# An attention and spectral-filter kernel: values turned and a bound summed on VectorE, low parts subtracted on GpSimd, and one filter piece's products ahead of the branch

## The chip, the cores and the metric

The kernel runs on one core of a Trainium2 chip. The metric is the time of one execution on the device, in microseconds (us); before the change it is 625.97 us, the median of 3 runs (625.66 to 625.98). The engines are TensorE (PE in the profile; its weight loads are listed as PEld), VectorE (DVE), ScalarE (ACT), GpSimd (POOL) and SyncE (SP, which only issues transfers). A name with a q behind it (PEldq, DVEq) is the engine's sequencer, which takes instructions in order, waits for their semaphores, loads registers and branches. TensorE writes to PSUM, which has eight banks of 128 x 512 float32.

## The reference

Two independent halves, put side by side. The first is attention with 16 heads of 28 columns that share one set of keys and values; the second multiplies a two-dimensional spectrum by a filter.

```python
# A: S = 2048, D = 448, H = 16, Dh = 28; wq and wk are eight times as large as the other weights
q = (x @ wq).reshape(B, S, H, Dh).transpose(0, 2, 1, 3)
k, v = x @ wk, x @ wv
p = softmax(einsum("bhqd,bkd->bhqk", q, k) * Dh ** -0.5)
a = einsum("bhqk,bkd->bhqd", p, v).transpose(0, 2, 1, 3).reshape(B, S, H * Dh) @ wo
# B: w_r, w_i of S x (D/2 + 1)
b = irfft2(rfft2(x) * (w_r + 1j * w_i), s=(S, D))
out = concatenate([a, b], axis=-1)
```

## The kernel before, in words

**Numbers in two parts.** TensorE multiplies in a fast mode that keeps fewer bits of a float32. Inputs, weights, keys and queries are therefore split into a high part (a cast) and a low part (the value less its high part, the helper `low`, L281), and a product is summed from three: high by high, high by low, low by high.

**Before the branch (about 5 to 69 us).** The input x comes in four chunks of 512 rows (c = 0 to 3) and four slices of columns (j = 0 to 3). For each chunk the high parts `xh` are cast (VectorE for c = 0, else ScalarE) and the low parts `xl` are subtracted on VectorE (L281). TensorE then makes the projections (L330): four groups of four heads, whose spare rows carry the columns of keys and values. ScalarE evicts each to `qraw` (L334) and VectorE takes the largest magnitude of each row (L335). Transfers from the SP and POOL queues gather keys and values into `kf` (L477), rows 0 to 31 the keys, 32 to 63 the values. Keys are split per half of 1024 columns: ScalarE casts (`keys_cast`, L276), VectorE subtracts (`keys_low`, L281), and SP copies the result to the three other strips of 32 partitions (`keys_strip`, L491). The first half is done ahead of the branch, the second behind it.

In between, the forward transform of the filter half runs in eight pieces q: VectorE folds the input (`fold_part`, L143 to L151), TensorE makes features from the folds (`features`, L161, one call for p = 0 and one for p = 1, each of e = 0 and 1), ScalarE copies them (L430), TensorE multiplies them by twiddles (`fft1_mm`, L171, into two banks), the result is copied out (`fft1_evict`, L186 on ScalarE or L188 on VectorE) and stored by SP (`fft1_store`, L192). Pieces 0 to 5 are done whole before the branch. Piece 6 (`L` in the code) and piece 7 have their features before it, and their L171 behind it, in `first_fill`.

**A bound per row.** Instead of the largest score of each row, the kernel subtracts a bound: the sum over a head's columns of |q| times |k| by their maxima. VectorE multiplies the maxima (`terms`, L496), TensorE sums over the 28 rows of a head with a matrix of ones and zeros `blk` (`shift`, L502), VectorE copies the sum to `cvec` (`bound`, L505), once for the first chunk and once for the other three. The largest of all sums is found by a reduce (L603), four small products that bring it to one partition (`tops`, L620), and a reduce to the single number `bits` (L621). Every engine loads `bits` into a register (`values_load`, L607) and branches (L635): where the bound is too large, a slow exact loop runs. With these inputs it does not.

**Values.** The value product wants the values with rows as keys: 16 blocks of 32 x 128 are transposed by TensorE against a unit matrix (L592: four, eight and four), collected in one bank, and copied to `vs` by VectorE behind the branch (L665).

**The order.** Before the branch each unit of work is a task with an engine, an assumed duration, the tasks it waits for and, where given, a due time. TensorE's tasks stay in the order of the code; for the other engines a small planner picks, among the tasks that could start first, the one due first. Behind the branch the order is written out by hand and by a running account of planned times (`clk`, and `free` for seven of the banks): the first strips of scores, the pieces' L171, value products, filter work.

**Behind the branch.** The scores of 512 queries and 128 keys make a step: four strips of 32 rows side by side (L1169, three products each, four banks), exponentials on ScalarE (L1185 for one bank, L1183 for two neighbours), and the value products of the step before last (L1218) into bank 7. `first_fill` puts the L171 of pieces 6 and 7 behind the first and the second step, in a free bank and bank 7, and its copies (L188) on VectorE. About 80 such steps are followed by groups in another form (L1146), mixed with the rest of the filter and the output projection (L1071). The spectrum's transform and its inverse are long chains on VectorE in the background.

## Time and profile before

| what | us |
|---|---|
| median of the runs | 625.97 |
| span of the profiled execution, first to last instruction | 624.6 |
| what the median has beyond that span | 1.37 |
| TensorE busy | 619.0 (99%) |
| ScalarE busy | 541.0 (87%) |
| VectorE busy | 344.1 (55%) |
| GpSimd busy | 90.7 (15%) |

The profiled execution's time is its span and what lies around it, for which the profile has no row of its own. A row of the timeline or of the chain gives start, length, engine, line and operation, what is written and read, and in brackets the idle time of the engine before it and what ended that. A matmul row's length is modelled and overlaps the next one. A row of the groups gives a count, the busy time, and the mean of one in ns. TensorE's granted clock is 1.00 all along.

### The profile page before, as it was taken

How to read it: one execution, taken by the hardware profiler on the slowest of the kernel's cores; microseconds unless marked ns; L12 is line 12 of the kernel's file. 1: busy time of each engine (PE TensorE's matmuls, PEld its weight loads, DVE VectorE, ACT ScalarE, POOL GpSimd, SP SyncE). 2: the span in 40 equal slices, each digit the busy share in tenths (PEclk: the TensorE clock that was granted, in tenths of full speed). 3: DMA queues.
4: the chain of work that ended last, by engine and by line, in shares of the span. 5: the costliest groups of instructions: out<-in, count | busy, mean ns of one | idle time of the engine just before them, and what ended most of it. 6: DMA issues, size and time to landing. Idle time of an engine off the chain costs nothing.

```text
span 624.6 us, 13634 instructions
## 1 busy us (share of the span) xinstructions
PE 619.0 (99%) x5367; PEld 319.4 (51%) x5367; DVE 344.1 (55%) x685; ACT 541.0 (87%) x977; POOL 90.7 (15%) x168
## 2 busy tenths in 40 slices
PE   9999999999999999999999999999999999999997
PEld 7877633333333346654345565656653346564335
DVE  6999604979698987897732513227451231321014
ACT  4645799999999998889999888878889998888993
POOL 1021130102121101020321210030210101020200
PEclk9999999999999999999999999999999999999999
DMA  8856794001123331171664242294213131016001
GB/s 304 276 134 171 193 247 185 16 20 46 34 90 88 87 76 47 40 161 28 211 213 104 77 119 78 61 215 147 82 60 94 34 98 34 16 66 149 18 1 59
DMA packets 28748, 65.31 MB, mean 105 GB/s; under 512 B 6514, under 2 KB 15826, under 8 KB 27270
## 3 DMA queue, kind: packets, MB, share of 16 engines
q1 hardware_dynamic: 21066, 43.25, 24.9%
q0 software_dynamic: 7472, 20.96, 11.3%
q8 instruction: 42, 0.69, 0.5%
q10 hardware_dynamic: 144, 0.23, 0.1%
q14 instruction: 24, 0.19, 0.1%
HBM read 30.35 MB, written 16.30 MB: 75 GB/s over the span
## 4 chain that ended last, share of the span: by engine, by line
PE 98%; ACT 1%; DMA 1%; DVE 0%; issue 0%; DVEq 0%; ACTq 0%
PE banks L1218 39%; PE banks L1146 21%; PE banks L1169 18%; PE banks L330 7%; PE banks L1071 6%; PE banks L973 2%; PE banks L161 2%; PE banks L999 2%; PE banks L171 1%; DMA raw<-xw 1%; ACT p L1185 0%; PE banks L592 0%; DVE bs L188 0%; PE banks L502 0%; ACT al L615 0%
## 5 line engine op out<-in xcount | busy, mean ns | idle before, releaser
L1203 ACT ACTIVATE p<-banks 128x512 f32<-128x512 f32 x512 | 256.5, 702 | 39.4 <-PE banks L1218 18.3
L1218 PE MATMUL banks<-p,vs 128*32 128x512 f32 x2048 | 254.5, 600 | 0.2 <-DVE bs L188 0.2
L1185 ACT ACTIVATE p<-banks 128x512 f32<-128x512 f32 x262 | 145.5, 614 | 1.5 <-PE banks L1169 1.2
L1146 PE MATMUL banks<-qa,ka 128*128 128x512 f32 x512 | 145.7, 407 | 0.0
L1183 ACT ACTIVATE p<-banks 128x1024 f32<-128x1024 f32 x125 | 129.3, 1034 | 0.0
L1146 PEld LDWEIGHTS banks<-qa,ka 128*128 128x128 f32 x512 | 90.6, 188 | 53.3 <-ACT p L1203 34.5
L1218 PEld LDWEIGHTS banks<-p,vs 128*32 128x32 f32 x2048 | 49.3, 108 | 112.4 <-issue 108.7
L1028 DVE COPY qraw<-banks 128x512 f32<-128x512 f32 x15 | 10.4, 691 | 68.6 <-PE banks L1218 68.6
L1033 POOL DMA_DIRECT2D sd<-qraw x15 | 8.9, 596 | 244.1 <-DVE qraw L1028 244.1
L1075 DVE COPY ya<-banks 128x448 f32<-128x448 f32 x12 | 7.5, 624 | 52.2 <-PE banks L1071 36.4
L1041 POOL DMA_DIRECT2D R<-rd x60 | 30.4, 513 | 39.4 <-DMA rd<-rs 36.5
L1169 PE MATMUL banks<-qa,oh 32*128 32x512 f32 x384 | 35.6, 443 | 0.0
L1169 PE MATMUL banks<-qa,kh 32*128 32x512 f32 x384 | 35.5, 443 | 0.0
L856 DVE SCALAR_TENSOR_TENSOR X<-w,X 128x226 f32<-128x226 f32 (+2 forms) x72 | 34.1, 473 | 2.4
L1169 PEld LDWEIGHTS banks<-qa,kh 32*128 32x128 f32 x384 | 14.5, 183 | 40.3 <-ACT p L1185 40.3
L1169 PEld LDWEIGHTS banks<-qa,oh 32*128 32x128 f32 x384 | 14.6, 183 | 38.5 <-ACT p L1185 37.7
L981 DVE CAST zh<-banks 113x512 fp32r<-113x512 f32 (+1 forms) x16 | 11.0, 685 | 27.9 <-ACT p L1203 27.0
L1005 DVE COPY w<-banks 128x256 f32<-128x256 f32 x16 | 6.8, 423 | 35.0 <-PE banks L999 31.9
L334 ACT ACTIVATE qraw<-banks 128x512 f32<-128x512 f32 x16 | 9.4, 599 | 17.8 <-PE banks L330 17.7
L330 PE MATMUL banks<-xh,wqh 128*128 128x512 f32 x64 | 24.3, 412 | 0.2 <-DVE xh L278 0.2
L1071 PE MATMUL banks<-woh,oh 128*128 128x448 f32 x64 | 23.6, 369 | 0.0
L1071 PE MATMUL banks<-wol,oh 128*128 128x448 f32 x64 | 23.1, 362 | 0.0
(139 smaller groups left out, 754.6 us busy)
## 6 DMA issues: line engine op xcount, KB each, us to landing
xb<-xb SPq DMA_DIRECT2D x8, 512.0 KB
qa<-qa SPq DMA_DIRECT2D x8, 512.0 KB
ob<-yo SPq DMA_DIRECT2D x16, 256.0 KB
X<-t POOLq DMA_DIRECT2D x8, 452.0 KB, 15.5
wf<-w POOLq DMA_DIRECT2D x8, 452.0 KB, 3.9
c<-t POOLq DMA_DIRECT2D x8, 452.0 KB, 4.4
R<-rd POOLq DMA_DIRECT2D x60, 56.0 KB, 2.4
t<-bs SPq DMA_DIRECT2D x14, 226.0 KB
```

Of the source, the lines that this page charges most:

```text
L161: mm(pa[r0:r0 + 32, e, 113 * k:113 * k + 113], f[:, 2 * r + k, 2 * p + e, h], cs1[:, 2 * r + k], start=True, stop=True)
L330: mm(pq[c, g], w[:, j, gs], x[:, j], start=(j == 0 and n == 0), stop=(j == 3 and n == 1))
L856: todo(226 * n, lambda d=d, q=q: STT(both(d), t[0].rearrange("p r n f -> p r (n f)"), q, both(a), op0=ALU.mult, op1=ALU.add))
L973: mm(pz[:w, j], fb["c2", q % 2][:, e, j, :w], fb["fi", q % 2][:, j], start=True, stop=True)
L1041: nc.gpsimd.dma_start(R[32 * i:32 * i + DH], rd[i:i + 1].to_broadcast([DH, CW]))
L1071: mm(p, x[c][:, g, s], w[:, m], start=(g == 0 and n == 0), stop=(g == NG - 1 and n == 2))
L1146: mm(bank[b], ka[:, kc * 128:(kc + 1) * 128], qa[c, g][:, h], start=True, stop=True)
L1169: mm(bank[bs[i]], k[r, kc * 128:(kc + 1) * 128], q[r], start=(n == 0), stop=(n == 2))
L1183: nc.scalar.activation(ends[1], banks[:, bs[1]:bs[1] + 2], AF.Exp, scale=SCALE)
L1185: nc.scalar.activation(pt[4 * st + i], bank[bs[i]], AF.Exp, scale=SCALE)
L1203: nc.scalar.activation(p, bank[b], AF.Exp, scale=SCALE)
L1218: mm(bank[7][32 * i:32 * i + 32], vs[:, kc], pt.pop(4 * st + i), start=(kc == 0), stop=(kc == 15))
```

## The change

Turning the values and summing the bound leave TensorE. VectorE transposes in blocks of 32 x 32: four instructions turn blocks 0 to 11 ahead of the branch, four small ones the last four behind it, straight into `vs`. The bound is a transpose, a sum, and a transpose back; the largest of the last result needs one product in `tops` instead of four. GpSimd subtracts the low parts of the third and fourth chunk (slices 0 to 2) and of both halves of the keys. The L171 of piece 6 moves from `first_fill` to the end of the work ahead of the branch; its copy and its two stores come first behind the branch. The products of piece 5 now stand before the features of piece 7, and these features' last part is split around `tops`: e = 0 ahead of it, the register load and e = 1 behind it. The constant `blk` and its load are gone, the starting values of `clk` and `free` are changed.

```diff
-            l = add(DVE, 0.61, lambda: low(out, lambda: xr[c, j][r], lambda: xs[c][0][r, j]), h)
+            pool = c > 1 and j < 3
+            l = add(POOL if pool else DVE, 1.6 if pool else 0.61,
+                    lambda: low(out, ..., nc.gpsimd if pool else nc.vector), h)
 ...
         def keys_low(h):
-            low(lambda: kl[:32, hs], lambda: kf[:32, hs], lambda: kh[:32, hs])
+            low(lambda: kl[:32, hs], lambda: kf[:32, hs], lambda: kh[:32, hs], nc.gpsimd)
 ...
-        def shift(c0, c1):
-            pb = small[c0] = spin(NG, c1 - c0)
-            mm(pb.rearrange("p g c -> p (g c)"), cons["blk"], prod[:, :, c0:c1], start=True, stop=True)
-        def bound(c0, c1):
-            nc.vector.tensor_copy(cvec[:, :, c0:c1], small[c0])
+        def shift(c0, c1, due, *deps):
+            def go():
+                terms(c0, c1)
+                nc.vector.transpose(across, prods)
+                nc.vector.tensor_reduce(sums[:, DH:DH + 1], across[:, :DH], axis=AX.X, op=ALU.add)
+                nc.vector.transpose(shifts, sums)
+                if c0:
+                    nc.vector.tensor_reduce(cmax, shifts, axis=AX.X, op=ALU.max)
+            return add(DVE, 0.85 if c0 else 0.65, go, kmb_, *smz, *deps, *(reds[a, b] for a in range(c0, c1) for b in range(NG)), due=due)
 ...
-                    kd = add(DVE, 1.1, lambda: keys_low(0), kc)
+                    kd = add(POOL, 3.0, lambda: keys_low(0), kc)
 ...
-        ts = add(DVE, 0.2, lambda: terms(1, NC), ...)
-        def turn_values(bs):
-            for b in bs:
-                nc.tensor.transpose(turned[0][:, b], kf[32:64, b * 128:(b + 1) * 128], cons["ident"][32:64, 32:64])
-        tv = add(PE, 0.3, first_values, ...)
-        cv = small_bank(0.2, lambda: shift(1, NC), 0.16, lambda: bound(1, NC), ts, blk_, tv)
+        fm_task(L - 1)
+        def turn_values(a, c0, c1):
+            x = kf[32:64, 128 * c0:128 * c1].rearrange("p (c a k) -> p a c k", a=4, k=32)
+            nc.vector.transpose(vs[32 * a:32 * a + 32, c0:c1], x[:, a])
+        cm = shift(1, NC, 60.0, cv0)
+        for a in range(4):
+            add(DVE, 0.5, lambda a=a: turn_values(a, 0, 12), *krow_, *fetched["v"][:7], cm if a == 3 else None)
         fa_task(L + 1, 0)
-        def last_values():
-            small["rv"] = nc.values_load(bits.bitcast(I32)[0:1, 0:1])
-            ...
-            features(pas[L + 1, 1], ff[L + 1], fc["cs1"][:113], 1)
-            turn_values(range(12, 16))
+        def last_features(e):
+            if e:
+                small["rv"] = nc.values_load(bits.bitcast(I32)[0:1, 0:1])
+            else:
+                ...
+            features(pas[L + 1, 1], ff[L + 1], fc["cs1"][:113], 1, (e,))
 ...
         def tops():
-            for g in range(NG):
-                mm(pb[0:1, 4 * g:4 * g + 4], cmax[:, g:g + 1], cons["sel4"], start=True, stop=True)
-        fm_task(L - 1)
-        tv = add(PE, 0.61, lambda: turn_values(range(4, 12)), fm[L - 1])
+            mm(pb[0:1, 0:4], cmax, cons["sel4"], start=True, stop=True)
+        lv = add(PE, 0.43, lambda: last_features(0), fa[L + 1][0], users[-6])
+        bt_ = small_bank(0.15, tops, 0.15, lambda: nc.vector.tensor_reduce(bits, small["t"][0:1, 0:4], axis=AX.X, op=ALU.max), cm, sel4_)
+        low_q["deps"].append(bt_)
-        lv = add(PE, 0.9, last_values, tv, kc, bt_, ...)
+        lv = add(PE, 0.43, lambda: last_features(1), bt_, lv)
         add(ACT, 0.5, last_evict, lv, kc)
+        add(PE, 0.85, lambda: pbs.update({L: fft1_mm(L)}), lv, *outs[L - 1])
 ...
-        nc.vector.tensor_copy(vs, turned[0])
+        fft1_out(L, pbs[L])
         keys_low(1)
+        for a in range(4):
+            turn_values(a, 12, 16)
         for p in (1, 2, 3):
             keys_strip(1, p)
 ...
-    clk = {"pe": 0.0, "dve": 1.9, ...}
-    free[turned[1]], free[turned[2]] = 0.8, 0.4
+    clk = {"pe": 0.0, "dve": 2.3, ...}
+    free[last_bank[0]], free[6] = 0.4, 0.9
 ...
-            if k < 2:
-                first_fill(L + k)
+            if not k:
+                first_fill(L + 1)
```

## The prediction

> **What bounds the kernel now.** I read the page's chain by engine first, then the chain in order of time around the branch.

> ```profile
> PE 98%; ACT 1%; DMA 1%; DVE 0%; issue 0%; DVEq 0%; ACTq 0%
> ```

> TensorE (PE) holds 98% of the chain. So a TensorE instruction taken away counts in full, unless TensorE then waits for something it did not wait for before. The rows of the chain from the last projection to the first strip of scores (start, us, what):

> ```profile
> 59.70 0.32 PE banks L502 x2
> ...
> 62.62 1.69 PE banks L161 x64
> 64.31 0.36 PE banks L592 x4
> 64.67 0.32 PE banks L502 x2
> 64.99 0.90 PE banks L161 x31
> 65.90 0.17 PE banks L620 x7
> 66.07 0.92 PE banks L171 x16
> 67.00 0.61 PE banks L592 x8
> 67.60 0.96 PE banks L161 x32
> ...
> 68.58 0.56 ACT al L615
> ...
> 69.17 0.98 PE banks L1169 x10
> ```

> The reader is to see that each piece begins where the last ends: no idle TensorE here. L592 turns the values, L502 sums the bound, L620 finds its top, L171 makes a filter piece's products, L161 their features, L1169 the first strip. The last four turnings (L592) are missing: from 68.56 to 69.17 the chain goes through ScalarE's copy of the last features (L615), and they lie beside that.

> What stands between the top of the bound and the branch is a register load, by line and in order of time:

> ```profile
> L607 PEldq TENSOR_LOAD <-bits x1: 986/986/986, 66.3 to 66.3; - x1
> L635 DVEq EVENT_SEMAPHORE  x1: 21/21/21, 68.0 to 68.0; - x1
> ...
> 65.73 0.35 PE L620 MATMUL banks<-sel,cmax 128*1 128x4 f32 x8
> 66.11 0.16 DVE L621 TENSOR_REDUCE bits<-banks 1x1 f32<-1x16 f32 x1
> ```

> The bits are written at 66.27, TensorE's sequencer loads them at once, and that takes 0.99 us, until 67.29. Nothing of it shows as idle time, because 24 matmuls (L171 and eight of L592, 1.53 us) had been handed to the array already. The whole way from the first L620 matmul to the end of the load is 1.56 us, and this cover is what the change rearranges.

> Behind the branch, ScalarE and TensorE:

> ```profile
> 69.52 1.20 DVE L281 TENSOR_TENSOR kl<-kf,kh 32x1024 fp32r<-32x1024 f32 x1
> 70.14 4.76 ACT L1185 ACTIVATE p<-banks 128x512 f32<-128x512 f32 x9 [1.00 <-PE banks L1169]
> 72.17 1.21 PE L171 MATMUL banks<-al,fwl 64*64 64x226 f32 x16
> 73.25 1.16 DVE L188 COPY bs<-banks 128x452 f32<-128x452 f32 x2 [0.91 <-ACT p L1185]
> 73.31 0.51 PE L1169 MATMUL banks<-qh,kh 32*128 32x512 f32 x4
> 74.47 1.06 PE L1218 MATMUL banks<-p,vs 128*32 128x512 f32 x8 [0.19 <-DVE bs L188]
> 74.79 1.02 ACT L1183 ACTIVATE p<-banks 128x1024 f32<-128x1024 f32 x1
> 76.95 1.02 ACT L1183 ACTIVATE p<-banks 128x1024 f32<-128x1024 f32 x1
> ...
> 78.85 1.02 ACT L1183 ACTIVATE p<-banks 128x1024 f32<-128x1024 f32 x1
> 80.82 1.02 ACT L1183 ACTIVATE p<-banks 128x1024 f32<-128x1024 f32 x1
> 81.72 1.10 ACT L1185 ACTIVATE p<-banks 128x512 f32<-128x512 f32 x2
> 82.72 1.02 ACT L1183 ACTIVATE p<-banks 128x1024 f32<-128x1024 f32 x1
> ```

> From 70.14 on ScalarE evicts without a break. Its step of four banks costs 0.90 for the double (80.82 to 81.72) and 1.00 for two singles (to 82.72), 1.90 together, the cadence of the steps (80.82 to 82.72). So TensorE and ScalarE run level here. The start is rougher: from 70.14 to 74.79 nine singles took 4.65 where 9 x 0.50 = 4.50 would do, the next steps took 2.16, 1.90 and 1.97. That is 0.15 + 0.26 + 0.07 = 0.48 us lost behind the branch, where two filter pieces are squeezed between the strips and the first value products (L1218) wait for the second one's copy (L188).

> **The change part by part.** *Taken off TensorE, ahead of the first strip:* L502 twice, 0.32 + 0.32; the turnings, 0.36 + 0.61 + 0.36 (the last four as the first four); L620 from four products to one, three quarters of 0.17, 0.12. Sum 2.09 us.

> *Moved:* the seventh piece's L171, 0.92, from behind the first strip to ahead of it. Its bank wait is for ScalarE's copies of the piece before, now made about 2 us earlier. Its two stores go ahead of the key strips on SP's queue.

> *The load's cover.* In the new order TensorE has: fifth piece's L171, features, half of the last features, the top, load, other half, the moved L171, branch. All that covered the load now stands before the top or behind the load. The load, two matmuls' latency and the bits' reduce are in the open: 1.56 less the 0.12 that two passes instead of eight save and the 0.05 that those two take, so 1.39 us idle. Bounds: nothing, if the matmuls behind the load did not wait for it, and 1.6. I take 1.39, since TensorE's queue is one queue in order and 0.99 is its own row. What queues behind the load: 32 matmuls and the branch; what waits for them: ScalarE's last feature copy, VectorE's piece copy, the first strip.

> *First strip:* 69.17 - 2.09 + 1.39 + 0.92 = 69.39, 0.22 later than before.

> *Behind it:* one filter piece fewer stands between the first strip and the value products. On TensorE that gives back 1.14 (72.17 to 73.31): L1218 at 74.47 + 0.22 - 1.14 = 73.55, 0.92 earlier. On ScalarE it can give back only the 0.48 of rough steps: 0.48 - 0.22 = 0.26 earlier. Both have the same cadence in the steps that follow, so the gain lies from 0.26 to 0.92, nearer to ScalarE's end, since ScalarE is the one without idle time here. I take 0.40. If the piece's copy were late again, L1218 would be the next to wait, as it is now.

> *Low parts on GpSimd.* Rows of the groups, then two windows (start:end, length, busy us of PE, PEld, DVE, ACT, POOL):

> ```profile
> L281 DVE TENSOR_TENSOR xl<-raw,xh 128x512 fp32r<-128x512 f32 x12 | 8.1, 686 | 0.3 <-ACT xh L276 0.2
> L281 DVE TENSOR_TENSOR kl<-kf,kh 32x1024 fp32r<-32x1024 f32 x2 | 2.4, 1202 | 0.0
> L1359 POOL TENSOR_TENSOR ol<-qraw,oh 128x128 fp32r<-128x128 f32 x3 | 1.4, 459 | 25.4 <-ACT oh L1356 25.4
> L236 POOL MEMSET kf<- 64x2048 f32 x1 | 1.8, 1802 | 0.1
> L258 POOL MEMSET wql<- 64x512 f32 x1 | 0.5, 519 | 0.3 <-POOLq L1474 0.3
> L1352 DVE STREAM_SHUFFLE r<-qraw 128x128 f32<-128x128 f32 x4 | 1.2, 301 | 0.0
> ```
> ```profile
> 16.00:57.00 41.00, 41.00 (x510) 32.24 (x508) 38.72 (x74) 21.89 (x41) 4.17 (x8) 1.00 0.65 192
> 80.00:90.00 10.00, 10.00 (x111) 3.43 (x108) 1.02 (x2) 10.00 (x17) 3.31 (x7) 1.00 1.03 249
> ```

> The two memsets give a fixed 0.09 us. With it, 459 ns is 2.87 ns a column, so 512 columns are 1.56 and 1024 are 3.03. Bounds: at the memsets' 0.84 ns a column beyond 128, 0.78 and 1.2; in proportion, 1.84 and 3.67. Six low parts and the first half's keys are 12.4 us of POOL (5.9 to 14.7) for 6 x 0.69 + 1.20 = 5.3 us off VectorE. Cover:

> ```profile
> 16.82 0.64 ACT L276 ACTIVATE xh<-raw 128x512 fp32r<-128x512 f32 x1
> ...
> 27.94 0.39 PE L330 MATMUL banks<-xl,wqh 128*128 128x512 f32 x1
> ...
> 62.92 0.42 DVE L151 TENSOR_TENSOR f<-xb 113x256 f32<-113x256 f32 x1
> 63.29 0.69 DVE L335 TENSOR_REDUCE qmx<-qraw 128x1 f32<-128x512 f32 x1
> ```

> The third chunk's high part is there at 17.46 and its low part is wanted at 27.94: 10.5 us for three parts of 1.56. Cost nothing; without cover, TensorE would wait for each part's excess. The second half's keys come after the branch. GpSimd passes it no later than VectorE, 1.73 after the bits (66.27 to 68.0), so near 68.5 in the new order, and the keys end at 71.5 against 69.52 + 1.20 = 70.72. The six strip copies behind them on SP's queue, with the two stores now ahead, start about 1 us later; the ninth step wants them, eight steps of 1.90 after the first strip, so nothing. GpSimd's loads of the output weights wait 3.03 behind the keys; VectorE, which casts the weights and would wait for them in order, is busy for only 1.02 of the 10 us from 80 on, so nothing again. Without that cover the next groups' queries would be late by as much.

> *Turned values and sums on VectorE.* No transpose is in this trace. Between the 0.17 of a small reduce and a 0.69 copy of 512 columns I take the shuffle's 0.30 for small ones and 0.5 for 384 columns. The last sum is five dependent instructions, 0.9 to 1.7 us, after the last reduce (63.29 + 0.69 - 0.32 for the L502 gone = 63.66): ready by 65.4 at the latest. The top's matmul comes at 62.62 - 0.32 + 1.69 + 0.92 + 0.90 + 0.48 = 66.29, so 0.9 us cover it, and past that each us of VectorE's lateness is one of TensorE's. VectorE does 4 x 0.5 more for the turning and sheds the 0.69 copy behind the branch.

> Sum: -0.40 us on a span of 624.6, 624.2. The span is 1.35 below the median of 625.97, which I keep: 625.6. A change under 0.2% (1.25 us, 624.72 to 627.22) can't be told from none here.

> **Rivals.** *VectorE falls behind (slower).* VectorE is 38.7 busy of 41 us from 16 to 57, 2.3 free, and its last fold ends (63.34) 1.6 before the features that read it (64.99). If its two-input instructions cannot run beside GpSimd's, it gains 12.4 us of blocking and 2.2 of turning and sums, loses 5.3: 9.3, against 3.9 of room, and TensorE waits 5.4 for folds: 631. Fifteen reduces like the one at 63.29 (0.69 each, 10.4 of the 38.7) have one input, and with the casts I put that share at 30%; then it is 8.7 + 2.2 - 5.3 - 3.9 = 1.7: 627.3. It decides once VectorE lags by over 3.9. I price it at 628.5. For it: the windows are full and most of their DVE work is two-input; against it: the only POOL row that subtracts (L1359) has no two-input VectorE work beside it, so nothing here shows blocking.

> [...]

> *The load is covered after all (faster).* Then the first strip waits only for VectorE to pass its branch, 1.73 after the bits. These come at 66.29 + 0.42 = 66.71 (66.11 + 0.16 - 65.73, less 0.12), so the strip starts near 68.5, 0.9 earlier, and the whole gain is 1.3 with ScalarE's end of the interval and 1.8 with TensorE's: 624.7 to 624.2, at 624.5. For it: the load showed no idle time before; against it: 24 queued matmuls explain that.

> *The order behind the branch changes.* It is written out from planned bank times, which the change sets anew; a lost double costs 0.1, so some tenths either way, inside my own range.

> **How the numbers follow.** No change to speak of 0.50 (own range 624.8 to 626.6), VectorE behind 0.27, the load covered 0.23, nearly all of it under 624.72. The range 624.1 to 628.7 leaves out the worst of the blocking and the best of the start. Since the slower case begins at 627.3 and the faster one at 624.7, each sign's chance is its case's own, with 0.01 of the faster case left to no change.

> **What would show it.** Right: TensorE idle some 1.4 us ahead of the last half of L161, with the load's row inside; the first strip near 69.4; doubles every 1.90 at once; POOL rows of 1.6 and 3.0 us. Wrong: L281 or fold rows on VectorE stretched beside POOL's, folds ending after 65, or a first strip before 68.7.

## The result: 0.9% slower

The changed kernel takes 631.98 us (median of four runs, 630.14 to 632.42), the kernel before beside it 625.93 (625.66 to 625.98): a ratio of 1.0092, 95% interval 1.0078 to 1.0107. The forecast was 625.6 with a range to 628.7. The profiled execution took 631.68 us, with a span of 629.9.

Line numbers below are those of the changed kernel: the low parts are L284, the folds L144 to L152, features L162, a piece's products L172, the turning L597, the bound L500 to L511, its top L619, `bits` L621, the register load L607, strips L1170, exponentials L1184 and L1186, value products L1219. Experiments that insert lines shift the later ones by up to 10. The first features on TensorE come at 25.91 in the trace of before and at 25.12 in this one; that start differs by up to 1 us between executions, so stages are compared from it.

**The first loss, around 32 us.** The timeline of the changed kernel, rows of VectorE, GpSimd and TensorE:

```profile
17.19 4.39 POOL L284 TENSOR_TENSOR xl<-raw,xh 128x512 fp32r<-128x512 f32 x3 [13.97 <-ACT xh L279]
...
18.92 1.51 DVE L150 TENSOR_TENSOR f<-xb 113x256 f32<-113x256 f32 x1
20.36 1.51 DVE L151 TENSOR_TENSOR f<-xb 113x256 f32<-113x256 f32 x1
...
25.12 1.76 PE L162 MATMUL banks<-cs,f 113*32 113x113 f32 x64
...
26.43 4.75 POOL L284 TENSOR_TENSOR xl<-raw,xh 128x512 fp32r<-128x512 f32 x3 [4.84 <-ACT xh L279]
26.54 0.68 DVE L340 TENSOR_REDUCE qmx<-qraw 128x1 f32<-128x512 f32 x1
...
28.23 1.78 DVE L147 TENSOR_TENSOR xb<-f 113x512 f32<-113x512 f32 x1
30.05 1.40 DVE L149 TENSOR_TENSOR f<-xb 113x256 f32<-113x256 f32 x1
31.13 2.54 POOL L284 TENSOR_TENSOR kl<-kf,kh 32x1024 fp32r<-32x1024 f32 x1
31.38 2.58 DVE L150 TENSOR_TENSOR f<-xb 113x256 f32<-113x256 f32 x1
32.04 0.38 PE L162 MATMUL banks<-cs,f 113*32 113x113 f32 x2
...
33.88 0.41 DVE L151 TENSOR_TENSOR f<-xb 113x256 f32<-113x256 f32 x1
...
34.35 1.97 PE L162 MATMUL banks<-cs,f 113*32 113x113 f32 x44 [1.92 <-DVE f L151]
```

Fold instructions, which have two inputs, are stretched to about the length of the GpSimd subtract beside them: 1.51 us where one of the six takes about 1.5, and 2.58 (31.38 to 33.96) where the keys' takes 2.54 (31.13 to 33.67). L151 at 33.88, with GpSimd done, takes 0.41. The reduce at 26.54, which has one input, takes 0.68 beside the same subtracts, as it does without them (0.68 at 25.98 in the trace of before). TensorE starts the second piece's features at 32.04, lacks the last folds, and stands still until 34.35.

The windows of the changed kernel around that wait (start:end, length, busy us of PE, PEld, DVE, ACT, POOL, then the granted clock) and around the branch:

```profile
35.00:36.00 1.00, 1.00 (x32) 1.00 (x28) 1.00 (x3) 0.22 (x1) 0.00 (x0) 0.53 0.76 186
36.00:37.00 1.00, 1.00 (x26) 0.84 (x18) 0.96 (x2) 0.33 (x1) 0.00 (x0) 0.50 0.94 328
37.00:38.00 1.00, 1.00 (x18) 0.57 (x15) 0.97 (x3) 0.55 (x1) 0.00 (x0) 0.50 0.34 127
38.00:39.00 1.00, 1.00 (x13) 0.53 (x6) 0.97 (x3) 0.18 (x1) 0.00 (x0) 0.77 0.01 4
...
73.00:74.00 1.00, 0.81 (x11) 0.16 (x4) 0.23 (x1) 0.00 (x0) 1.00 (x1) 0.50 0.93 212
74.00:75.00 1.00, 1.00 (x11) 0.91 (x12) 0.97 (x3) 0.00 (x0) 0.90 (x2) 0.50 0.88 202
75.00:76.00 1.00, 1.00 (x14) 0.31 (x9) 0.96 (x4) 0.48 (x1) 1.00 (x2) 0.50 0.30 70
```

Behind each of two waits the granted clock is 0.50 for a while. In the first, 0.47 + 0.50 + 0.50 + 0.23 = 1.70 us of full clock are missing, so it lasted 3.4 us (3.41 in the trace's record of the clock). In the trace of before the clock is 1.00 throughout.

**The second loss, at the branch.** The changed kernel's timeline, the bound's last sum to the first value products:

```profile
69.39 0.19 DVE L511 TENSOR_REDUCE cmax<-cvec 128x1 f32<-128x32 f32 x1
69.61 0.57 DVE L597 STREAM_TRANSPOSE vs<-kf 32x384 f32<-32x384 f32 x1
69.63 0.19 PE L619 MATMUL banks<-sel,cmax 128*1 128x4 f32 x2
...
70.21 0.15 DVE L621 TENSOR_REDUCE bits<-banks 1x1 f32<-1x4 f32 x1
71.69 0.60 PE L162 MATMUL banks<-cs,f 113*32 113x113 f32 x16 [1.86 <-issue]
...
72.21 1.47 PE L172 MATMUL banks<-al,fwl 64*64 64x226 f32 x16
...
73.87 0.91 PE L1170 MATMUL banks<-qh,kh 32*128 32x512 f32 x4 [0.19 <-PEq L634]
...
75.52 4.71 ACT L1186 ACTIVATE p<-banks 128x512 f32<-128x512 f32 x9 [2.63 <-PE banks L1170]
...
79.21 1.07 PE L1219 MATMUL banks<-p,vs 128*32 128x512 f32 x8
```
```profile
L607 PEldq TENSOR_LOAD <-bits x1: 1228/1228/1228, 70.4 to 70.4; - x1
```

TensorE waits 1.86 us between the top and the last half of the features. The reduce that writes `bits` starts 0.4 us after the end of its product (69.63 + 0.19), since a turning (69.61 to 70.18) stands in front of it on VectorE; the load then takes 1.23 us. Behind it the moved products run at half clock: 1.47 us, where the sixteen of the piece before, at 67.30, take 0.99.

Counted from the first features, in us (start of the first row of each):

| | before | after | later by |
|---|---|---|---|
| third piece's features (38.17; 41.44) | 12.26 | 16.32 | 4.06 |
| first strip (69.17; 73.87) | 43.26 | 48.75 | 5.49 |
| first value products (74.47; 79.21) | 48.56 | 54.09 | 5.53 |

So three quarters of the loss arise at the second piece's folds: 2.3 us of waiting and 1.75 of half clock. The rest arises at the load. What follows the first strip comes neither earlier nor later.

### The profile page after: what moved, and what is told of

Read it like the earlier page. It is cut to its first block, busy times and chain, and to the rows that moved or that the text cites. A ratio compares the mean times of both kernels' runs of the same rounds, so it can differ in the third digit from the quotient of the medians.

```text
span 629.9 us, 13598 instructions
## 1 busy us (share of the span) xinstructions
PE 620.4 (99%) x5341; PEld 318.9 (51%) x5341; DVE 349.6 (56%) x688; ACT 540.8 (86%) x977; POOL 104.9 (17%) x178
## 4 chain that ended last, share of the span: by engine, by line
PE 88%; ACT 0%; issue 0%; ACTq 0%
PE banks L1219 39%; PE banks L1147 20%; PE banks L1170 19%; PE banks L1072 6%; PE banks L974 2%; PE banks L1000 2%; PE banks L172 0%; ACT p L1186 0%; ACT yb L1083 0%; ACTq L1083 0%
## 5 line engine op out<-in xcount | busy, mean ns | idle before, releaser
L1204 ACT ACTIVATE p<-banks 128x512 f32<-128x512 f32 x512 | 256.5, 694 | 39.6 <-PE banks L1219 18.5
L1219 PE MATMUL banks<-p,vs 128*32 128x512 f32 x2048 | 254.5, 600 | 0.0
L1186 ACT ACTIVATE p<-banks 128x512 f32<-128x512 f32 x262 | 155.5, 691 | 3.0 <-PE banks L1170 2.6
L1184 ACT ACTIVATE p<-banks 128x1024 f32<-128x1024 f32 x125 | 139.6, 1117 | 0.0
L1219 PEld LDWEIGHTS banks<-p,vs 128*32 128x32 f32 x2048 | 49.3, 108 | 112.3 <-issue 108.8
L1029 DVE COPY qraw<-banks 128x512 f32<-128x512 f32 x15 | 10.4, 692 | 66.7 <-PE banks L1219 66.7
L1170 PE MATMUL banks<-qa,oh 32*128 32x512 f32 x384 | 35.7, 443 | 0.0
L1170 PE MATMUL banks<-qa,kh 32*128 32x512 f32 x384 | 35.5, 443 | 0.0
L1170 PEld LDWEIGHTS banks<-qa,kh 32*128 32x128 f32 x384 | 14.5, 183 | 40.3 <-ACT p L1186 40.3
L1170 PEld LDWEIGHTS banks<-qa,oh 32*128 32x128 f32 x384 | 14.6, 183 | 38.5 <-ACT p L1186 37.7
L335 PE MATMUL banks<-xh,wqh 128*128 128x512 f32 x64 | 23.8, 402 | 0.2 <-DVE xh L281 0.2
```

The lines of the kernel that those rows point to most:

```text
L335: mm(pq[c, g], w[:, j, gs], x[:, j], start=(j == 0 and n == 0), stop=(j == 3 and n == 1))
L1170: mm(bank[bs[i]], k[r, kc * 128:(kc + 1) * 128], q[r], start=(n == 0), stop=(n == 2))
L1184: nc.scalar.activation(ends[1], banks[:, bs[1]:bs[1] + 2], AF.Exp, scale=SCALE)
L1186: nc.scalar.activation(pt[4 * st + i], bank[bs[i]], AF.Exp, scale=SCALE)
L1204: nc.scalar.activation(p, bank[b], AF.Exp, scale=SCALE)
L1219: mm(bank[7][32 * i:32 * i + 32], vs[:, kc], pt.pop(4 * st + i), start=(kc == 0), stop=(kc == 15))
```

## Experiment 1: who holds the folds

Two kernels put low parts back on VectorE.

```diff
# low parts of inputs back (both kernels)
-            pool = c > 1 and j < 3
+            pool = False
# low parts of keys back as well (the first kernel alone)
-            low(lambda: kl[:32, hs], lambda: kf[:32, hs], lambda: kh[:32, hs], nc.gpsimd)
+            low(lambda: kl[:32, hs], lambda: kf[:32, hs], lambda: kh[:32, hs])
-                    kd = add(POOL, 3.0, lambda: keys_low(0), kc)
+                    kd = add(DVE, 1.1, lambda: keys_low(0), kc)
```

> The changed kernel with every low part (third and fourth chunk, both halves of the keys) back on VectorE; all else as changed. Theory A (GpSimd's subtracts keep VectorE's two-input folds from running, and TensorE's two long idle spells each halve its clock for 3.41 us): no fold row over 0.7 us, no wait of TensorE for the fold near 32 us, one halved-clock spell instead of two; 632.0 - 2.3 - 1.7 = 628.0 us. Theory B (the folds are late because the planner orders VectorE differently and VectorE has the turning and sums to do): still 631 to 632.5.

> The changed kernel with the six low parts of the inputs back on VectorE, the keys' low parts still on GpSimd. Theory A: VectorE is held up only beside the one subtract of 2.5 us for the first half of the keys, less than the room its folds have (4.9 us for the second fold): no wait for the fold, 627.5 to 628.3 us. Theory B: 631 to 632.5.

With all low parts on VectorE: 628.4 us (627.7 to 630.11), ratio 1.0042 (1.003 to 1.0055), near the 628.0 of theory A. The wait for folds is gone; the third piece's features come 38.35 - 26.10 = 12.25 after the first, as in the kernel before. More than half of the loss was GpSimd's. With the keys alone on GpSimd: 629.31 (626.75 to 631.78), 1.0052 (1.0031 to 1.0072), which does not stand clear of the first and misses theory A's 627.5 to 628.3. No fold is late at the second piece, but TensorE waits 0.76 and 0.29 us for folds of the last piece (until 65.04 and 65.71); why these are late was not traced. Its runs lie 5 us apart, which their mean granted clocks (0.994 to 0.999) explain only in part. Its timeline shows the same hold from the other side:

```profile
29.83 5.73 POOL L284 TENSOR_TENSOR kl<-kf,kh 32x1024 fp32r<-32x1024 f32 x1 [26.61 <-ACT kh L279]
...
33.36 2.76 DVE L284 TENSOR_TENSOR xh<-raw,xh 64x512 fp32r<-64x512 f32 x1
```

GpSimd's one subtract takes 5.73 us (2.54 in the changed kernel) while VectorE runs one two-input instruction after another, and then VectorE's takes 2.76 instead of 0.69. What is left in the first kernel stands around the top of the bound:

```profile
67.10 0.57 DVE L597 STREAM_TRANSPOSE vs<-kf 32x384 f32<-32x384 f32 x1
67.13 0.19 PE L619 MATMUL banks<-sel,cmax 128*1 128x4 f32 x2 [0.61 <-DVE cmax L511]
67.70 0.15 DVE L621 TENSOR_REDUCE bits<-banks 1x1 f32<-1x4 f32 x1
68.77 0.98 PE L162 MATMUL banks<-cs,f 113*32 113x113 f32 x16 [1.45 <-DVE bits L621]
```

TensorE waits 0.61 for the sum and 1.45 for the load.

## Experiment 2: is it GpSimd's work, or its reading

The kernel before, with work on GpSimd whose result nobody reads (into a tile `by`): six subtracts of the size of the moved ones, or memsets of about the same length at the same points of the program. VectorE keeps all its own work. Line numbers here are those of the kernel before, up to 3 higher.

```diff
# the first kernel
+            if c > 1 and j < 3:
+                add(POOL, 1.6, lambda: nc.gpsimd.tensor_tensor(by, xr[c, j], xs[c][0][:, j].bitcast(F32), op=ALU.subtract), h)
# the second kernel
+            if c > 1 and j < 3:
+                add(POOL, 1.6, lambda: [nc.gpsimd.memset(by, 0.0) for _ in range(3)], h)
```

> The kernel before, plus six GpSimd subtracts of 128 x 512 into a scratch tile that nothing reads, at the points where the change has GpSimd subtract; VectorE still does all its own. Theory A: VectorE's folds beside them grow from 0.42 and 0.68 to over 1 us, and as VectorE keeps its own six low parts (4.1 us) it lags more than in the changed kernel: TensorE waits for folds 2 to 5 us and its clock halves once, 629 to 633 us. Theory B: work that nothing waits for costs nothing, 626 us.

> As the run before it, but GpSimd only writes: three memsets of 128 x 512 (0.52 us each) in place of each subtract, about the same GpSimd time. If what is contended is a read of SBUF by GpSimd, nothing grows: 625.9 to 626.2 us. If any GpSimd work on SBUF holds VectorE's two-input instructions up: as the run before it.

Subtracts: 629.77 us (629.22 to 630.21), ratio 1.0061 (1.0044 to 1.0077). Memsets: 625.94 (625.74 to 626.62), ratio 1.0004 (0.9994 to 1.0013). The timeline of the kernel with subtracts, its waits by engine and line (us in total, times, longest), and the timeline of the kernel with memsets:

```profile
17.72 4.73 POOL L303 TENSOR_TENSOR by<-raw,xh 128x512 f32<-128x512 f32 x3 [14.59 <-ACT xh L277]
17.81 1.79 DVE L146 TENSOR_TENSOR xb<-f 113x512 f32<-113x512 f32 x1
...
26.89 3.17 DVE L143 TENSOR_TENSOR f<-xb 113x512 f32<-113x512 f32 x2
```
```profile
PE banks L505 <- DVE prod L499: 1.4, 2, 0.9
PE banks L161 <- DVE f L148: 1.3, 1, 1.3
```
```profile
3.06 11.08 POOL L303 MEMSET by<- 128x512 f32 x18
...
9.46 0.69 DVE L282 TENSOR_TENSOR xl<-raw,xh 128x512 fp32r<-128x512 f32 x1
...
10.67 0.67 DVE L279 CAST xh<-raw 128x512 fp32r<-128x512 f32 x1
```

Six subtracts that compute nothing for anyone cost 3.9 us, although VectorE's instructions up to the branch stand in the same order as in the kernel before: so it is not the order in which the planner puts the tasks. The memsets did not run where the subtracts do. They wait for no input, so GpSimd ran all eighteen from 3.06 to 14.14 us, before VectorE's first fold (15.60). The unchanged time therefore does not show what a GpSimd that only writes would cost beside the folds. What the trace does show is VectorE's work beside the memsets: subtracts with two inputs take 0.69 us, as in the kernel before (0.69), while its four casts of `xh` take 0.65 to 0.72 instead of 0.42 to 0.43. So beside these memsets VectorE's two-input instructions are not held up, and beside GpSimd's subtracts they are (1.78 us for a subtract of VectorE at 19.52 in the kernel with subtracts, instead of 0.69). The two GpSimd instructions differ in more than the reading (a subtract also computes, and is three times as long); that it is GpSimd's reading of SBUF was not tested by itself.

Put together, the rows are: two-input folds of 1.51 and 2.58 us beside a subtract, two-input instructions of unchanged length (0.69 us) beside memsets, and 5.73 us for the GpSimd subtract that begins, at 29.83, while one of VectorE's is running (29.50 to 30.18). In the kernel with subtracts TensorE waited without the clock ever falling (mean granted clock 1.000), where theory A had expected one halved stretch.

## Experiment 3: what the idle stretches cost beside themselves

Matmuls that nobody reads are put where TensorE waits: into the changed kernel at both places, and into the first kernel of experiment 1 at the load.

```diff
+        def busy(n):
+            nothing = spin(512) if n < 18 else bank[7]
+            for _ in range(n):
+                mm(nothing[:, :256], idle[:, :128], idle, start=True, stop=True)
...
# ahead of the second piece's features (the changed kernel alone)
+                    if q == 1:
+                        add(PE, 0.0, lambda: busy(20), m)
# between the top and the load (both)
+        add(PE, 0.0, lambda: busy(16), bt_["deps"][0])
```

> The changed kernel with matmuls that nobody reads (256 columns, into a bank that is free then): 20 of them ahead of the second piece's features, where TensorE waited 2.3 us for folds, and 16 between the top of the bound and the register load, where it waited 1.86 us. Theory C (an idle TensorE of some 2 us makes the clock halve for one stretch of 3.41 us, which costs 1.7 us each time, on top of the wait): the folds are stretched and the waits last as long as before, but the clock stays at 1.0 throughout, and the time is 632 - 2 x 1.7 = 628.6. Theory D (only the waits themselves cost; the halved clock lies beside other work): the time stays at 632, or rises where a matmul of the filler is in the way.

> The changed kernel with all low parts back on VectorE, and 16 matmuls that nobody reads between the top of the bound and the register load. Theory C: no halved clock any more, so 628.4 less 1.7 (one halved stretch) to 3.4 (two), 625.0 to 626.7, near the kernel before. Theory D: 628.4 as without the filler.

The changed kernel, filled: 630.28 us (629.42 to 631.77), ratio 1.0074 (1.0055 to 1.0093). Its timeline and one window:

```profile
32.15 2.36 PE L427 MATMUL banks<-idle 128*128 128x256 bf16 x20
...
34.44 1.96 PE L162 MATMUL banks<-cs,f 113*32 113x113 f32 x64
...
68.72 0.19 PE L627 MATMUL banks<-sel,cmax 128*1 128x4 f32 x2 [0.58 <-DVE cmax L517]
```
```profile
36.00:37.00 1.00, 1.00 (x32) 0.66 (x22) 0.97 (x2) 0.77 (x2) 0.00 (x0) 1.00 0.98 315
```

The folds are as late as they were, and the clock stays at 1.00. From the first features (25.32) the third piece's come at 39.97, after 14.65 us instead of 16.32: the 1.67 that theory C gives one halved stretch. But the top then waits 0.58 for the sum of the bound, for which it had not waited: the halved clock had given VectorE time to catch up. At the first value products (77.10, 51.78 after the first features) 2.31 of the expected 3.4 are left. The spans agree: 627.6 to 628.7 in its four runs, 628.4 to 630.6 in those of the changed kernel, medians 2.2 apart; the medians of the times are 1.7 apart, since two of these runs took some 3 us around the span instead of 1.8. By the ratios to the kernel before, 1.0092 and 1.0074, it is 1.1 us, and their intervals overlap, so in this kernel the gain rests on the spans and the timeline.

The other kernel, filled: 627.53 (627.22 to 628.21), ratio 1.0023 (1.0013 to 1.0032), against 1.0042 without. That is 1.2 us less (0.0019 of 626) for matmuls that do no work, where theory C had 1.7 to 3.4 and theory D none; all ten runs lie below D's 628.4, and the clock stayed at 1.00 in the profiled one. The ten runs now lie within 1 us. Without the filling the six lay within 2.4, and their mean granted clock went with the time: 627.7 to 628.44 us at 0.997 and 0.998, 629.81 and 630.11 at 0.994 and 0.995. One halved stretch of 3.41 us lowers the mean over 626 us by 0.0027. This fits one halved stretch more in some executions than in others, at the same wait.

## Experiment 4: real work as the load's cover

All low parts but the keys' second half are back on VectorE. The top goes ahead of piece 5's products and of both halves of the last features, the load behind these. Only one turning stays ahead of the branch.

```diff
+        add(DVE, 0.5, lambda: turn_values(0, 0, 12), *krow_, *fetched["v"][:7])
...
         bt_ = small_bank(0.15, tops, ...)
+        fm_task(L - 1)
+        lv = add(PE, 0.43, lambda: last_features(0), fa[L + 1][0], users[-6])
+        lv = add(PE, 0.43, lambda: last_features(1), lv)
+        add(PE, 0.1, load_bits, bt_, lv)
         add(PE, 0.85, lambda: pbs.update({L: fft1_mm(L)}), lv, *outs[L - 1])
...
# behind the branch
-            turn_values(a, 12, 16)
+            turn_values(a, 0 if a else 12, 16)
```

> The changed kernel with all low parts but the keys' second half back on VectorE, and real work as the load's cover: the top of the bound goes ahead of the sixth piece's products and of both halves of the last features, the load behind these; twelve turned blocks of values ahead of the branch, the rest behind it. Theory C with the load in the open as the cause of what remains: no halved clock, no idle TensorE over 0.5 us before the first strip, the first strip near 68.3 and 624.0 (1.9 faster than the kernel before). Rival: the turnings that now stand behind the branch, and the last fold, hold up VectorE's copy of the seventh piece, and the value products come no earlier than before: 625.9.

625.81 us (625.27 to 626.42) beside 626.22 (625.58 to 626.66): ratio 0.9992 (0.9983 to 1.0002), no difference that can be told, and nearer to the rival's 625.9 than to 624.0. The timeline, TensorE and VectorE:

```profile
65.74 0.19 PE L615 MATMUL banks<-sel,cmax 128*1 128x4 f32 x2 [0.92 <-ACT al L435]
65.86 0.99 PE L172 MATMUL banks<-a,fw 64*64 64x226 f32 x16
...
69.07 0.51 PE L1170 MATMUL banks<-qh,kh 32*128 32x512 f32 x4 [0.16 <-PEq L634]
...
70.01 2.45 DVE L596 STREAM_TRANSPOSE vs<-kf 32x128 f32<-32x128 f32 x4
...
72.49 1.16 DVE L189 COPY bs<-banks 128x452 f32<-128x452 f32 x2
...
73.18 0.51 PE L1170 MATMUL banks<-qh,kh 32*128 32x512 f32 x4 [1.05 <-DVE bs L189]
...
74.08 1.06 PE L1219 MATMUL banks<-p,vs 128*32 128x512 f32 x8
```

The load no longer stops TensorE, and the clock stays at 1.00. But the top waits 0.92 for the bound's sum (the profile names an older copy; `cmax` was ready 0.1 before the start). The first strip comes 43.22 after the first features (25.85), against 43.26 before, and not near 68.3. The 2.45 us of turnings behind the branch keep the copy waiting, and TensorE 1.05 with it, as the rival had it; the first value products still come 0.33 earlier than in the kernel before (48.23 against 48.56).

Two more kernels take these waits away: the turnings stand right behind the bits on VectorE, half of the last features ahead of the top; the second of them also puts the load behind the moved products.

```diff
+        for a in range(1, 4):
+            add(DVE, 0.6, lambda a=a: turn_values(a, 0, 16), bt_, *fetched["v"])
+        add(DVE, 0.3, lambda: turn_values(0, 12, 16), bt_, *fetched["v"])
# the second kernel: behind the products, and behind the turnings (tv)
-        add(PE, 0.1, load_bits, bt_, lv)
+        add(PE, 0.1, load_bits, lm, *tv)
```

> As the run before with real work behind the top, but the other turnings (three of 16 blocks, one of 4) stand on VectorE right behind the bits, ahead of the branch, where VectorE was idle for 2.1 us, and the first half of the last features stands ahead of the top. Theory (what was left there is the 1.05 us in which TensorE waited for a copy of the seventh piece behind the turnings, and the 0.92 us ahead of the top): both waits fall to 0.5 us or less together, no halved clock, first value products 1 us earlier or more; 0.9 to 1.5 us less than that run, 624.7 in its terms, a ratio of 0.9975 to the kernel before. Rival: the turnings only move the wait to VectorE's copy ahead of the first strip or to its register load, and the ratio stays at 0.999.

> As the other run of this pair, but the register load stands behind the moved seventh products on TensorE and behind all turnings on VectorE, so the moved products cover it too. Theory: no matmul is queued behind the load any more, the wait inside it is gone (0.1 to 0.4 us), the branch comes when the products end or when the load ends, whichever is later: a ratio of 0.997. Rival: VectorE and the other engines load later, so the branch is passed later there and the first strip's eviction waits: 0.9985.

625.75 us (625.4 to 626.36) and 626.13 (625.7 to 626.62) beside 625.89: ratios 0.9997 (0.9988 to 1.0006) and 1.0003 (0.9994 to 1.0013). The times are nearer to the rivals' 0.999 and 0.9985 than to the theories' 0.9975 and 0.997. The timeline of the first of the two:

```profile
67.65 1.44 PE L172 MATMUL banks<-al,fwl 64*64 64x226 f32 x16 [0.31 <-ACT bs L187]
...
69.25 0.51 PE L1171 MATMUL banks<-qh,kh 32*128 32x512 f32 x4 [0.16 <-PEq L637]
...
73.97 1.06 PE L1220 MATMUL banks<-p,vs 128*32 128x512 f32 x8
```

The copy's wait is gone, and yet the first value products come 48.20 after the first features (25.77), the same as in the kernel ahead of this pair (74.08 - 25.85 = 48.23): the moved products now wait for the bank that ScalarE's copy of piece 5 has to free and take 1.44, so the first strip is at 43.48, 0.26 later than there, and that eats what the copy gave. That is a wait which neither the theory nor the rival had named. In the second, the first strip waits 0.35 for VectorE's branch, close to its rival (which named the strip's eviction), and stands at 43.51. No order tried brings the first strip more than 0.04 earlier than the kernel before has it. None beats the kernel before by what can be measured.

## Why the prediction was wrong, step by step

**The step that failed** is "Low parts on GpSimd", in its sentence "Cost nothing" for the third chunk's parts. It counted how long GpSimd takes, 1.56 us each against 10.5 of room, and asked who waits for GpSimd's results. The durations were right: 1.5 us each (4.39 and 4.75 for three). Nobody waited for them. What it costed at nothing is what GpSimd does to VectorE while it works. The prediction had this as its first rival and gave it 0.27 because no row of before showed a blocked instruction. Taking the low parts back recovered 3.1 us (the ratios 1.0092 and 1.0042, of 626), and subtracts alone cost 3.9.

**The rival's price.** It put the loss at 1.7 to 5.4 us of waits for folds, from 12.4 us of blocking against 3.9 of room over the whole stage. Measured: one wait of 2.3 us at the second piece, none later. A sum over 41 us was the wrong measure of the room. What counts is the room of the folds that are due next: the second piece's, at 32 us, beside which four of the seven subtracts fall. The rival had no term for the clock, which added 1.75 us there. So even the rival that had the right rows, as priced at 628.5, fell short.

**The load in the open** had the right place and the wrong size: 1.39 us forecast, 1.86 measured. The load itself took 1.23 instead of 0.99 (0.24 more), and `bits` came 0.31 late (ready 0.73 us after the top's start, 0.42 forecast), behind a turning that the step did not have queued there, though the change ties it to the sum (`cm if a == 3`). The two exceed the difference of 0.47 since the profile counts its 1.86 from the modelled end of the top's two products, 0.19 long, where the sum took 0.05. The half clock behind the load, 0.48 us on the moved products (1.47 against 0.99), was not in the sum. The clock's costs here and at the folds come from one error: a wait on TensorE was priced as its length. In the kernel with all low parts on VectorE, filling this wait with idle matmuls made it 1.2 us faster.

**The sum ready by 65.4, with 0.9 us to spare.** In the first kernel of experiment 1, where GpSimd holds nothing up, the top waits 0.61 for it. The five instructions took 1.2 us, inside the 0.9 to 1.7. But VectorE reached them later than the step had it: a turning stood right ahead of them (65.30 to 65.87; 0.57 each where 0.5 was forecast).

**The first strip** was forecast 0.22 later. With GpSimd's hold, the top's wait and the clock it came 5.49 later. The parts taken off TensorE (2.09) and moved (0.92) did what was said: the second filled kernel of experiment 3, with all low parts on VectorE, has its strip 44.90 after the first features, 1.64 later than before, and shows a wait of 0.61 for the top and a stretch of 2.14 from the top to the rest of the features. With the top's own 0.05, the sum is -2.09 + 0.92 + 0.61 + 2.09 = 1.53.

**Behind the branch** the forecast took a gain of 0.40 with the first strip 0.22 later, so 0.62 less between the first strip and the value products (0.48 to 1.14 by its two sides). That stretch was 5.30 before. It was 4.56 in the filled changed kernel and 4.72 and 4.78 in the second and third kernels of experiment 4, so 0.74, 0.58 and 0.52 less, near what was taken; it was 5.01 in the first kernel of experiment 4 and 5.08 in the second filled kernel, where TensorE waited for VectorE's copy. In the changed kernel it was 5.34, with the second halved stretch across it: the clock took what the move gave.

**The rival "the load is covered"** (624.5) was tested in experiment 4: its condition was met and its gain did not come, since the top then waited for VectorE's sum, and the moved products for a bank. **The order behind the branch** was not at work: the steps are 1.90 again from 81.23 on.

**What would show it wrong** named the right rows: folds stretched beside POOL's, and they were.

## What to carry to other kernels

## What the runs showed of the hardware that was not expected

**The clock.** In profiled executions, TensorE waits of 1.86 and 1.92 us (changed kernel; the second is the 2.3 at the folds without the two products that began it), of 1.67 (keys on GpSimd, where the products behind it take 1.70 instead of 0.99) and of 0.61 and 1.45 close together (low parts on VectorE) were followed by halved clock. In the changed kernel each halved stretch lasts 3.41 us; with the low parts on VectorE the clock is 0.71 in the window from 68 to 69, 0.50 in each from 69 to 75 and 0.88 in the next, so 6.8 us, two such lengths in a row. Waits of 1.3 us and less (experiments 2 and 4) were not followed by it: the mean granted clock of those executions is 0.999 or 1.000. In the changed kernel the two stretches begin at 35.05 and 72.60 us (the clock is 0.53 in the window from 35 to 36 and 0.80 in that from 72 to 73), 37.55 apart, eleven times their length; what that means was not tested. In the kernel with subtracts, waits of 1.3 and 0.2 us for folds had no halved stretch behind them, and the 1.67 had one. What decides it for a wait in between, or from one execution of a kernel to the next, was not tested.

**The register load.** The same load on TensorE took 0.99 us in the kernel before, 1.23 in the changed one, 0.82 and 1.04 in the two of experiment 1, 1.32 in the second filled kernel and 0.49 in the first kernel of experiment 4. In the last, one other engine (ScalarE, 0.49 as well) was loading `bits` at the same time; in the five others two or more were. That is no test, and what sets it was not found.

**Open.** The subtracts of experiment 2 cost 3.9 us, of which 2.7 stand above as waits of TensorE for the fold and the terms, and 0.5 more as two short waits for VectorE (a fold, 0.2, and `qm`, 0.3); the rest was not traced.

**Casts.** Beside GpSimd's memsets VectorE's casts of `xh` took 0.65 to 0.72 us instead of 0.42 to 0.43 (experiment 2). The kernel was no slower for it (ratio 1.0004).
